# A block-diagonal 128x128 product done as four 64x64 products on the quarters of the array

## Chip, cores, metric

One core of a Trainium2 chip. The metric is device time in microseconds (us); each kernel ran several times and medians are given. The kernel before: 3359.38 us in the first three runs (3359.05 to 3360.88).

## The reference

```python
# x (8, 3008, 256); filt (1505, 256); w_in (256, 2048); w_out (2048, 256); all float32 in effect
X = np.fft.rfft(x, axis=1)
y = np.fft.irfft(X * (filt_r + 1j * filt_i)[None], n=3008, axis=1)
h = y.reshape(24064, 256) @ w_in
g = h * np.clip(h + 3, 0, 6) / 6
return g @ w_out
```

A Fourier transform along the tokens, a filter, the inverse transform, then an MLP.

## The kernel before

A transform of length 3008 = 47 x 64 goes in two stages. The first one, which the change touches, is a 64-point transform over n2 for each n1. The 48 (padded) values of n1 are n1 = 24 h + i with h = 0, 1. The two values of h lie on partitions 0 to 63 and 64 to 127, and the 24 values of i come in 6 chunks of 4. The weights `wa` are block-diagonal, the same 64x64 block twice, so half of the array multiplies by zero.

```python
wa[r, h * 64 + k2] = c                  # rows of h meet columns of h only; zero elsewhere
...
psF = pool("psF", 2, space=PSUM)        # two PSUM banks for all stages of the transform

def a_unit(b, i):                       # two values of i at a time
    c, r = divmod(i, XC // 2)
    ...
    ps = psF.tile([P, 2, D], FP32, name="psf", tag="f")
    nc.tensor.matmul(ps, wa, st["x", b, c][:, 2 * r:2 * r + 2, :], start=True, stop=True)
    nc.scalar.activation(out=st["t1", b, c][:, 2 * r:2 * r + 2, :], in_=ps, func=AXT.Copy)
    ...

def z_store(b, c):                      # to DRAM, where the next stage reads n1 along the partitions
    t = st.pop(("t1", b, c))
    for h in range(2):
        for ri in range(2):
            p0 = h * 64 + ri * 32
            r0 = ri * SL + h * H + c * XC
            nc.gpsimd.dma_start(z_d[b, :, r0:r0 + XC, :], t[p0:p0 + 32, :, :])

def down(b, m, jt):                     # second product of the MLP, four groups of tokens
    for q in ...:
        n = min(P, ntok(m) - q * P)     # 64 instead of 128 for q = 3 of the last block (448 tokens)
        nc.tensor.matmul(po[q // 2][0:n, q % 2, :], g[:, ds(q * P, n)], w_out[:, jt, :], ...)
```

The MLP of batch b runs in 96 slots: `up` (two matmuls of 512 columns), what the plan puts there of the transform of batch b + 1, `down` (four matmuls of 256). The first stage of batch b + 1 stands in every second slot from 0 to 22; the last stage of the inverse transform (`n_unit`) in slots 6, 8, 22, 24 and so on. Batch 0's transform runs ahead of the loop, beside the conversion of the weights. I call that stretch the start.

## Time and profile before

| | before |
|---|---|
| device time | 3359.38 us |
| profiled span | 3356.7 us |
| start, until the first MLP product | 237.07 us |
| one batch in the loop (batches 1 to 6 of the trace, first `up` to next first `up`) | 395.13 us |
| last batch, without a transform beside it | 345.57 us |
| tail, from the start of the last matmul to the end | 12.29 us |

The rows below the span are differences of start times read off the trace; together with the first batch (390.99) they fill the span. The batch is the row to read: inside it TensorE has no gap, so whatever lengthens or shortens TensorE's work changes it one to one. The prediction shows the lines.

Two words for what follows. A *record* is one matmul instruction in the trace; every f32 matmul of the code leaves two. A *visit* is a stretch in which TensorE works on less than the full 128x128 array, from the first such record to the next full-size one; what I call its price includes what the full-size records on both sides lose.

### The profile page before, as it was taken

To read this page: it belongs to the slowest core of one execution; us is meant where nothing else is said; L and a number is where in the kernel's file an instruction comes from. 1 tells how busy PE (TensorE), PEld (TensorE's weight loads), DVE (VectorE), ACT (ScalarE), POOL (GpSimd) and SP (SyncE) were. 2 spreads that over 40 slices of the span, in tenths; PEclk is the share of its full clock that TensorE was granted. 3 is DMA by queue.
4 is the path that set the end of the run, shared out by engine and by line. 5 is a ranking of instruction groups with operands and counts; after the bars stand their busy time and mean duration, and the time that the engine had idled before them with its cause. 6 is when DMAs were issued, how large, how long until landed. Compare 5 with 4: busy or idle time off the path is not lost.

```text
span 3356.7 us, 28371 instructions
## 1 busy us (share of the span) xinstructions
PE 3203.8 (95%) x11712; PEld 2117.0 (63%) x11712; DVE 919.8 (27%) x1413; ACT 740.8 (22%) x1137; POOL 218.2 (6%) x390
## 2 busy tenths in 40 slices
PE   1469999999999999999999999999999999999998
PEld 0246666666666676666675666666666666666665
DVE  2951232113321233112331133212332123311211
ACT  0012222222222222222222222222222222222221
POOL 2101000010001000010000100000000100000000
PEclk6579999999999999999999999999999999999999
DMA  8432121121212211021211212111111211010000
GB/s 149 140 100 77 32 60 39 37 58 47 55 29 62 52 45 44 24 74 47 65 28 44 62 37 63 32 55 46 52 44 29 74 43 43 24 36 19 19 7 12
DMA packets 76352, 168.20 MB, mean 50 GB/s; under 512 B 17410, under 2 KB 42244, under 8 KB 76032
## 3 DMA queue, kind: packets, MB, share of 16 engines
q0 software_dynamic: 32416, 86.55, 9.7%
q1 hardware_dynamic: 43808, 79.85, 9.2%
q8 instruction: 92, 1.51, 0.2%
q14 instruction: 36, 0.29, 0.0%
HBM read 91.29 MB, written 74.97 MB: 50 GB/s over the span
## 4 chain that ended last, share of the span: by engine, by line
PE 93%; DVE 3%; DMA 2%; issue 1%; POOL 0%; ACT 0%; SPq 0%; POOLq 0%; ACTq 0%
PE po L329 40%; PE psh L312 39%; PE psf L275 6%; PE psf L258 3%; PE psn L300 3%; PE psf L236 2%; DMA ft<-in_filt_i_dram 1%; DMA ft<-in_filt_r_dram 1%; DMA bits<-in_moe_w_in_dram 0%; DVE s L266 0%; DVE s L264 0%; DVE s L265 0%; DVE rest L213 0%; DVE rest L216 0%; DVE big L210 0%
## 5 line engine op out<-in xcount | busy, mean ns | idle before, releaser
L329 PE MATMUL po<-w_out,g 128*128 128x256 f32 (+1 forms) x6144 | 1471.9, 380 | 0.0
L312 PE MATMUL psh<-xn,w_in 128*128 128x512 f32 (+1 forms) x3072 | 1428.5, 587 | 0.0
L329 PEld LDWEIGHTS po<-w_out,g 128*128 128x128 f32 (+1 forms) x6144 | 1138.8, 188 | 398.9 <-issue 271.9
L317 DVE SCALAR_TENSOR_TENSOR g<-r,psh 128x512 f32<-128x512 f32 (+1 forms) x768 | 519.5, 676 | 2301.1 <-ACT r L316 2301.1
L316 ACT ACTIVATE r<-psh,half_c 128x512 f32<-128x512 f32 (+1 forms) x768 | 520.8, 678 | 2210.8 <-PE psh L312 2210.8
L312 PEld LDWEIGHTS psh<-xn,w_in 128*128 128x128 f32 x3072 | 573.8, 190 | 433.7 <-issue 399.2
L275 PE MATMUL psf<-s,wi 128*96 128x256 f32 x1024 | 261.6, 401 | 28.6 <-DVE s L266 28.1
L275 PEld LDWEIGHTS psf<-s,wi 128*96 128x96 f32 x1024 | 174.7, 173 | 131.9 <-issue 49.5
L236 PE MATMUL psf<-xc,wa 128*128 128x512 f32 x192 | 105.3, 639 | 76.2 <-ACT t L237 69.8
L258 PE MATMUL psf<-t,wb 96*128 96x256 f32 x512 | 139.3, 396 | 27.6 <-issue 19.0
L258 PEld LDWEIGHTS psf<-t,wb 96*128 96x128 f32 x512 | 98.5, 197 | 92.7 <-issue 67.5
L345 POOL DMA_DIRECT2D out_dram<-o x96 | 50.9, 535 | 1483.6 <-issue 1443.8
L300 PEld LDWEIGHTS psn<-wai,t 128*128 128x128 f32 x768 | 102.0, 194 | 52.6 <-issue 52.6
L280 ACT ACTIVATE t<-psf 96x512 f32<-96x512 f32 x128 | 75.9, 593 | 235.0 <-PE psf L275 235.0
L247 POOL DMA_DIRECT2D z_tmp<-t x192 | 93.4, 493 | 441.0 <-ACT t L237 414.9
L283 POOL DMA_DIRECT2D g_tmp<-t x64 | 44.6, 698 | 1069.6 <-ACT t L280 1068.6
L236 PEld LDWEIGHTS psf<-xc,wa 128*128 128x128 f32 x192 | 36.8, 203 | 117.8 <-ACT t L237 77.9
L300 PE MATMUL psn<-wai,t 128*128 128x128 f32 x768 | 102.6, 277 | 8.7 <-DMA t<-g_tmp 8.7
L264 DVE TENSOR_TENSOR s<-psf,ft 128x512 f32<-128x512 f32 x128 | 87.7, 685 | 15.2 <-PE psf L258 15.0
L266 DVE TENSOR_TENSOR s<-psf,ft 64x512 f32<-64x512 f32 x128 | 88.9, 695 | 1.8
L265 DVE TENSOR_TENSOR s<-psf,ft 64x512 f32<-64x512 f32 x128 | 87.4, 683 | 3.3
L237 ACT ACTIVATE t<-psf 128x512 f32<-128x512 f32 x96 | 56.9, 597 | 106.4 <-DMA z_tmp<-t 81.4
(34 smaller groups left out, 267.6 us busy)
## 6 DMA issues: line engine op xcount, KB each, us to landing
z_tmp<-t POOLq DMA_DIRECT2D x192, 128.0 KB, 3.6
t<-z_tmp SPq DMA_DIRECT2D x64, 384.0 KB, 3.9
g_tmp<-t POOLq DMA_DIRECT2D x64, 384.0 KB, 3.4
t<-g_tmp SPq DMA_DIRECT2D x192, 128.0 KB, 4.0
xc<-in_x_dram SPq DMA_DIRECT2D x88, 256.0 KB, 4.9
out_dram<-o POOLq DMA_DIRECT2D x88, 256.0 KB, 3.1
bits<-in_moe_w_in_dram POOLq DMA_DIRECT2D x8, 512.0 KB, 4.3
bits<-in_moe_w_out_dram POOLq DMA_DIRECT2D x8, 512.0 KB, 5.2
```

Of the source, the lines that this page charges most:

```text
L236: nc.tensor.matmul(ps, wa, st["x", b, c][:, 2 * r:2 * r + 2, :], start=True, stop=True)
L247: nc.gpsimd.dma_start(z_d[b, :, r0:r0 + XC, :], t[p0:p0 + 32, :, :])
L258: nc.tensor.matmul(ps[:, u, :], wb[k // KC][:, k % KC, :], st["t2", b, k // TC][:, k % TC, :], start=True, stop=True)
L264: nc.vector.tensor_tensor(out=s1, in0=ps, in1=f, op=ALU.mult)
L265: nc.vector.tensor_tensor(out=s2[0:HALF], in0=ps[0:HALF], in1=f[HALF:P], op=ALU.mult)
L266: nc.vector.tensor_tensor(out=s2[HALF:P], in0=ps[HALF:P], in1=f[0:HALF], op=ALU.mult)
L275: nc.tensor.matmul(ps[0:KR, u, :], wi[k // KC][:, k % KC, q, :], ss[q][:, u, :], start=(q == 0), stop=(q == 1))
L300: nc.tensor.matmul(ps[:, ts(q, P)], st["t4", b, m][:, q, ts(dh, P)], wai, start=True, stop=True)
L312: nc.tensor.matmul(ps[:, 0:w], w_in[:, dt, ts(jt, P)], xn[:, dt, 0:w], start=(dt == 0), stop=(dt == 1))
L316: nc.scalar.activation(out=r[:, 0:w], in_=ps[:, 0:w], func=AXT.Relu, bias=half_c, scale=1.0 / 6.0)
L317: nc.vector.scalar_tensor_tensor(out=g[:, 0:w], in0=r[:, 0:w], scalar=1.0, in1=ps[:, 0:w], op0=ALU.min, op1=ALU.mult)
L329: nc.tensor.matmul(po[q // 2][0:n, q % 2, :], g[:, ds(q * P, n)], w_out[:, jt, :], start=(jt == 0 and q % 2 == 0), stop=(jt == JT - 1 and ...
```

## The change

The intent is to use the idle half of the array. Each 64x64 block becomes a product on a quarter of its own: rows h, columns g, where g selects which two of the chunk's four values of i. All four can then work at once on different data. The PSUM tile is now one for each h, with g on the partitions, so the stores change too: eight of 64 KB in place of four of 128 KB. The chunk's products stand in one slot instead of two.

```diff
-            wa[r, h * 64 + k2] = c
+            wa[r, k2] = wa[r, 64 + k2] = c
 ...
-    def a_unit(b, i):
-        ...
-        ps = psF.tile([P, 2, D], FP32, name="psf", tag="f")
-        nc.tensor.matmul(ps, wa, st["x", b, c][:, 2 * r:2 * r + 2, :], start=True, stop=True)
-        nc.scalar.activation(out=st["t1", b, c][:, 2 * r:2 * r + 2, :], in_=ps, func=AXT.Copy)
+    def a_unit(b, c):
+        xc = st.pop(("x", b, c))
+        t = t1p.tile([P, 2, XC // 2, D], FP32, name="t1")
+        ps = [psF.tile([P, 2, D], FP32, name="psf", tag="f") for h in range(2)]
+        for g in range(2):
+            for h in range(2):
+                nc.tensor.matmul(ps[h][ts(g, 64)], wa[ts(h, 64), ts(g, 64)],
+                                 xc[ts(h, 64), 2 * g:2 * g + 2, :], start=True, stop=True)
+        for h in range(2):
+            nc.scalar.activation(out=t[:, h, :, :], in_=ps[h], func=AXT.Copy)
+        st["t1", b, c] = t

     def z_store(b, c):
-        for h in range(2):
+        for g in range(2):
             for ri in range(2):
-                p0 = h * 64 + ri * 32
-                r0 = ri * SL + h * H + c * XC
-                nc.gpsimd.dma_start(z_d[b, :, r0:r0 + XC, :], t[p0:p0 + 32, :, :])
+                p0 = g * 64 + ri * 32
+                r0 = ri * SL + c * XC + 2 * g
+                for h in range(2):
+                    nc.gpsimd.dma_start(z_d[b, :, r0 + h * H:r0 + h * H + 2, :], t[p0:p0 + 32, h, :, :])
 ...
-            for i in range(12):
-                at(t + 2 * i, a_unit, n, i)
-                if i % 2: ...                       # z_store, x_load at t + 2 * i + 1
+            for c in range(NB):
+                at(t + 4 * c, a_unit, n, c)
+                at(t + 4 * c + 2, z_store, n, c)    # and x_load
```

More of the change, by code (lines that the diff above doesn't have):

```diff
@@ L49, in _make_tables @@
             c, s = np.cos(th), np.sin(th)
-            wa[r, h * 64 + k2] = c
+            wa[r, k2] = wa[r, 64 + k2] = c
             wai[h * 64 + k2, r] = c * (2.0 if k2 else 1.0)
             if k2:
-                wa[r, h * 64 + 32 + k2] = -s
+                wa[r, 32 + k2] = wa[r, 96 + k2] = -s
                 wai[h * 64 + 32 + k2, r] = -2.0 * s
@@ L56, in _make_tables @@
                 alt = 1.0 - 2.0 * (n2 % 2)
-                wa[r, h * 64 + 32] = alt
+                wa[r, 32] = wa[r, 96] = alt
                 wai[h * 64 + 32, r] = alt
@@ L229, in x_load @@
         st["x", b, c] = t
-    def a_unit(b, i):
-        c, r = divmod(i, XC // 2)
-        if r == 0:
-            st["t1", b, c] = t1p.tile([P, XC, D], FP32, name="t1")
-        ps = psF.tile([P, 2, D], FP32, name="psf", tag="f")
-        nc.tensor.matmul(ps, wa, st["x", b, c][:, 2 * r:2 * r + 2, :], start=True, stop=True)
-        nc.scalar.activation(out=st["t1", b, c][:, 2 * r:2 * r + 2, :], in_=ps, func=AXT.Copy)
-        if r == XC // 2 - 1:
-            st.pop(("x", b, c))
+    def a_unit(b, c):
[9 more added lines that the diff above has]
+        st["t1", b, c] = t
     def z_store(b, c):
         t = st.pop(("t1", b, c))
-        for h in range(2):
+        for g in range(2):
             for ri in range(2):
-                p0 = h * 64 + ri * 32
-                r0 = ri * SL + h * H + c * XC
-                nc.gpsimd.dma_start(z_d[b, :, r0:r0 + XC, :], t[p0:p0 + 32, :, :])
+                p0 = g * 64 + ri * 32
+                r0 = ri * SL + c * XC + 2 * g
+                for h in range(2):
+                    nc.gpsimd.dma_start(z_d[b, :, r0 + h * H:r0 + h * H + 2, :], t[p0:p0 + 32, h, :, :])
     def t2_load(b, c):
@@ L362 @@
         for c in range(NB):
-            a_unit(0, 2 * c)
-            a_unit(0, 2 * c + 1)
+            a_unit(0, c)
             z_store(0, c)
@@ L403 @@
                 continue
-            for i in range(12):
-                at(t + 2 * i, a_unit, n, i)
-                if i % 2:
-                    c = i // 2
-                    at(t + 2 * i + 1, z_store, n, c)
-                    if c + 3 < NB:
-                        at(t + 2 * i + 1, x_load, n, c + 3)
+            for c in range(NB):
+                at(t + 4 * c, a_unit, n, c)
+                at(t + 4 * c + 2, z_store, n, c)
+                if c + 3 < NB:
+                    at(t + 4 * c + 2, x_load, n, c + 3)
             for c in range(3):
```

## The prediction

> **What bounds the kernel now.** I read the page first (busy shares, slices, chain, groups), then the timeline of PE in the loop, the groups with shapes kept apart, and the timelines of POOL and DVE in the start. From the page:
>
> ```profile
> PE 3203.8 (95%) x11712; PEld 2117.0 (63%) x11712; DVE 919.8 (27%) x1413; ACT 740.8 (22%) x1137; POOL 218.2 (6%) x390
> PE   1469999999999999999999999999999999999998
> ...
> PEclk6579999999999999999999999999999999999999
> ...
> PE 93%; DVE 3%; DMA 2%; issue 1%; POOL 0%; ACT 0%; SPq 0%; POOLq 0%; ACTq 0%
> ...
> L236 PE MATMUL psf<-xc,wa 128*128 128x512 f32 x192 | 105.3, 639 | 76.2 <-ACT t L237 69.8
> ```
>
> PE is full from the fourth slice on at full clock and is 93% of the chain. Up to about 240 us there is a start of another kind (transform of batch 0, conversion of weights). So in the loop each us of PE order is a us of the result; in the start it is not. The stage that changes (L236) is 105 us of busy PE: 96 matmuls in the code (8 batches x 12), 192 records, so an f32 matmul is two pairs of weight load and matmul. Its 70 us of waiting for ACT lie in the start (13 waits in all, the longest 62 us). Only batches 1 to 7 pay in the loop: 7 x 6 = 42 chunks of two matmuls. The timeline of PE in the loop:
>
> ```profile
> 243.18 1.02 PE L236 MATMUL psf<-xc,wa 128*128 128x512 f32 x2
> 244.04 1.89 PE L329 MATMUL po<-w_out,g 128*128 128x256 f32 x8
> 245.76 1.88 PE L312 MATMUL psh<-xn,w_in 128*128 128x512 f32 x4
> 247.48 1.89 PE L329 MATMUL po<-w_out,g 128*128 128x256 f32 x8
> ```
>
> Starts count, not durations (they overlap). L236 takes 244.04 - 243.18 = 0.86 us for two records, 0.43 each; L312 takes 1.72 for four, again 0.43; L329 1.72 for eight of half width. No gap anywhere. A chunk costs 4 x 0.43 = 1.72 us, and 42 chunks 72 us: even removing the stage would gain 2.15%, and halving it 36 us, 1.1%.
>
> **What the skill says.** First, the Trainium skill, "TensorE: Matmul & The Clock Gate", Back-to-back issue gap, gives N / 2.4 + 2.5 ns, 216 ns for 512 columns; the trace has 430 for f32, so each of the two records streams its columns twice. The time follows the columns streamed, not rows or outputs used: a 64x64 product alone is no cheaper than a 128x128 one. Second, "TensorEngine Tiling (Array Packing)", Key Properties: tiles work in parallel, but changing the tiling mode drains the engine. Third, the first page, The mechanism (packing small matmuls): matmuls start and end strictly in program order, and a weight load runs beside matmuls in flight only where the row group differs. Of running side by side this trace shows nothing. Of changing mode it does, because the last token block has a product with 64 columns of weights:
>
> ```profile
> 597.71 1.77 PE L312 MATMUL psh<-xn,w_in 128*128 128x448 f32 x4
> 599.31 2.03 PE L329 MATMUL po<-w_out,g 128*128 128x256 f32 x8
> 601.28 1.77 PE L312 MATMUL psh<-xn,w_in 128*128 128x448 f32 x4
> ...
> L329 PEld LDWEIGHTS po<-w_out,g 128*64 128x64 f32 x256 | 24.4, 134 | 42.5 <-issue 42.5
> ```
>
> The first three are the timeline in the block of 448 tokens, the last the group of 64-column loads. Without a change of mode L312 would take 1.72 x 448/512 = 1.505 us and L329 1.72, together 3.23. From 597.71 to 601.28 it is 3.57: **0.34 us for one visit** to the 64-column mode, with two records in it. The two narrow records start 0.27 us apart (600.70 and 600.97 in a narrower window) where wide ones of 256 columns start 0.215 apart, so about 0.05 us is a second load that is not hidden in this mode. A visit is thus about 0.29 us, plus 0.05 for each further load into a tile just in use. This agrees with the second page in that leaving and re-entering the full mode costs something.
>
> **The change, part by part.**
> 1. PE, per chunk. Removed: two matmuls, 4 records, 1.72 us. Added: four matmuls, 8 records of the same 512 columns, 0.43 each, in the order (rows 0, columns 0), (rows 1, columns 0), (0,1), (1,1). The built program has 5952 matmuls against 5856, and 2 records each. All four quarters at once would be 2 x 0.43. But each product is a pair of records on one quarter, next to each other in the queue, and the second must wait for the first; as order is strict, nothing passes it. So: first of A; second of A beside first of B; second of B beside first of C; second of C beside first of D; second of D. That is **5 steps of 0.43 = 2.15 us**, not 2. Add 4 unhidden second loads, 4 x 0.05 = 0.2, and a visit, 0.29: 2.65 us. Against 1.72: +0.93 us a chunk, x 42 = **+39 us**.
> 2. Both PSUM buffers of the tag are taken in one slot instead of one in every second slot. In slot 8 of each batch the last-stage product (L300) stands in front and holds one of them: its eviction takes 0.6 us plus some 0.2 to start, while the second quarter product would want the buffer after 0.6. About 0.3 us, x 7 = +2 us. ACT has the same two evictions of 0.60 a chunk; it is 22% busy, so nothing.
> 3. Stores. Eight per chunk of 64 KB in place of four of 128 KB, 192 more POOL issues of 0.49 us = 94 us of POOL, which has 6% busy; in the loop the reader of this data comes four slots (over 14 us) after the last store is given, against 3.6 us to land. Nothing there. In the start the last chunk's stores are on the path:
>
> ```profile
> 105.14 0.56 POOL L188 DMA_DIRECT2D bits<-in_moe_w_in_dram x1 [3.86 <-DVE rest L213]
> 105.70 2.09 POOL L247 DMA_DIRECT2D z_tmp<-t x4
> ...
> 116.78 0.69 DVE L264 TENSOR_TENSOR s<-psf,ft 128x512 f32<-128x512 f32 x1 [3.96 <-PE psf L258]
> ```
>
> Timelines of POOL and DVE: four stores end at 107.8, the read starts at 110.7, and DVE, which then sets the pace until 206 us, has waited 3.96 us for it. Eight stores end 2 us later: **+2 us**. The chunks before are paced by DVE (6.5 us each, against 8 x 0.5 + 0.6 of POOL), so nothing more. The PE work of batch 0 hides beside DVE.
>
> Sum: 39 + 2 + 2 = +43 us, 3402. Loads of the next quarter might not be pulled ahead in full, which makes each of three steps up to 0.1 us longer (up to 12 us); I add 3 for that: **3405 us**, +1.4%.
>
> **The rivals.**
> - *No overlap at all*: f32 with its double passes, or this mode, lets only one quarter run. Then 8 x 0.43 + 7 x 0.05 + 0.29 = 4.10 us a chunk, +2.38, x 42 = +100, with the 4 us above 3463 us, +3.1%. For it: no record of the kernel before shows two matmuls together. Against: the skill measured such overlap, if not in f32. 23%.
> - *Full overlap*: all first records together, then all second ones: 2 x 0.43 + 0.05 + 0.29 = 1.20 us, -0.52, x 42 = -22, plus 4: 3341 us, -0.5%. It is what the change intends. Against: the pairs stand one after another and order is strict. 7%.
> - *A heavier visit*: changing rows and columns might drain longer than changing columns alone. Each 0.1 us more is 4 us; 0.6 us more would be needed to reach +2%. 5%.
> - *The start or DMA moves the result*: more and smaller packets where DMA is busiest (share 8 of 10 in the first slice). The stores of the first chunk stand behind filter and weight loads and may be some us later, but DVE's conversions do not wait for them. A few us at most.
>
> **Range and chances.** Main case 3402 to 3420, 65%; serial about 3463, 23%; full overlap about 3341, 7%; the rest between. Range 3378 to 3468. The line for +2% is 3426.6, for -2% 3292. Slower by over 2%: 23% plus a heavy visit, 0.28. Faster by over 2% would take more than the whole loop share of the stage: 0.01. Within 2%: 0.71.
>
> **What would show it.** In the changed kernel's PE timeline inside the loop: from the first record of the quarter products to the next L329 or L312-type product 2.65 us (main), 4.1 (serial) or 1.2 (full); second records of one quarter start within some 10 ns of first records of the next (main), all starts 0.43 or more apart (serial), four starts together (full). 384 records in the group. POOL at about 600 instructions, with 8 stores a chunk; first DVE product in the start at about 118.8 instead of 116.78; DMA and ACT still far from full. The prediction is wrong if PE idles in the loop on ACT or DMA by more than some us, if the visit costs much over 0.3 us, or if the start moves by more than about 5 us.

## The result

The changed kernel takes **3335.95 us** (3335.33 to 3336.33, 4 runs) against 3359.22 us (3357.64 to 3360.88, 4 runs): ratio 0.993, 95% interval 0.9916 to 0.9944. A ratio is the mean of one kernel's fast runs over the mean of the other's of the same rounds, so not quite the ratio of the medians. Results are correct. The prediction said 3405 and a range from 3378 to 3468: the sign was wrong. The mean granted clock is 0.973 before and 0.987 after, but only the start differs: from the first MLP product on it is 1.00 in both, and the last batch takes 345.57 us in both.

From the page of the changed kernel, busy time by engine and the group of the quarter products (its line is now L239):

```profile
PE 3185.7 (96%) x11904; PEld 2090.9 (63%) x11904; DVE 920.4 (28%) x1413; ACT 737.3 (22%) x1137; POOL 315.3 (9%) x582
...
L239 PE MATMUL psf<-xc,wa 64*64 64x512 f32 x384 | 67.0, 673 | 75.6 <-ACT t L242 70.6
```

Twice the records (384 against 192) in 67.0 us of busy time instead of 105.3. Records that run together count once in busy time. The waiting for ACT before it, 70.6 against 69.8 us, is the same: it lies in the start. The timeline of TensorE in the loop shows one visit (start and length in us, then the group; L317 is `up`, L334 `down`):

```profile
246.88 1.88 PE L317 MATMUL psh<-xn,w_in 128*128 128x512 f32 x4
248.69 1.09 PE L239 MATMUL psf<-xc,wa 64*64 64x512 f32 x8
249.71 1.99 PE L334 MATMUL po<-w_out,g 128*128 128x256 f32 x8
251.54 1.88 PE L317 MATMUL psh<-xn,w_in 128*128 128x512 f32 x4
```

Eight records of 512 columns from 248.69 to 249.71, **1.02 us**; at 0.43 us each, one after another, they would take 3.44. The neighbours pay for the change of mode: L317 takes 1.81 instead of 1.72 up to the visit, and L334 1.83 instead of 1.72 after it. In all, 246.88 to 251.54 is 4.66 us, less 3.44 for the neighbours: a chunk costs 1.22 us instead of 1.72. The starts of the records of another such visit, read off the trace (ns from the first; A to D are the quarters in the order of the code, "load" is the weight load of a record):

```
load A1 -2  load B1 5   load C1 12  load D1 18      first records of A, B, C, D start at 0, 7, 13, 20
load 2nd records   53  60  67  73                   second records            start at 480, 487, 493, 500
next product (full array) starts at 1019
```

All four first records run together, then all four second ones. That is the rival that the prediction called full overlap and gave 7%. Where the time went, from the same starts as in the table above:

| us | before | after | difference |
|---|---|---|---|
| start | 237.07 | 235.15 | -1.92 |
| seven batches with a transform beside them | 390.99 + 6 x 395.13 | 388.85 + 6 x 392.88 | -15.6 |
| last batch | 345.57 | 345.57 | 0 |
| tail | 12.29 | 7.53 | -4.8 |
| span | 3356.7 | 3334.4 | -22.3 |

Two things are left to explain. The loop gave back 15.6 us, not 42 x 0.50 = 21; and 4.8 us came from a tail that the change seems not to touch.

For the first: in slot 8 the visit follows a product of the last stage (L305). The timelines of TensorE and of its weight loads there:

```profile
264.48 1.05 PE L305 MATMUL psn<-wai,t 128*128 128x128 f32 x8
265.47 1.84 PE L239 MATMUL psf<-xc,wa 64*64 64x512 f32 x8
267.24 1.13 PE L334 MATMUL po<-w_out,g 128*128 128x256 f32 x4
```

```profile
265.47 0.19 PEld L239 LDWEIGHTS psf<-xc,wa 64*64 64x64 f32 x2
266.22 0.20 PEld L239 LDWEIGHTS psf<-xc,wa 64*64 64x64 f32 x6 [0.57 <-ACT xn L306]
```

This visit takes 1.77 us. Two loads are issued at once and six 0.75 us later, after ACT has emptied the bank that L305 used. The same lines answer a second question, namely what the queue looks like. The two early loads are both of quarter A (its first and its second record), so in the queue the two records of a product stand together, ahead of the wait that belongs to B. (A build of the kernel has them so: A1 A2 B1 B2 C1 C2 D1 D2.) Yet in an undisturbed visit B1, C1 and D1 start 7 to 20 ns after A1, and A2 only at 480 ns. **They pass A2.**

### The profile page after: what moved, and what is told of

It is laid out like the page before. It is cut to its first block, busy times and chain, and to the rows that moved or that the text cites. A ratio compares the mean times of both kernels' runs of the same rounds, so it can differ in the third digit from the quotient of the medians.

```text
span 3334.4 us, 29079 instructions
## 1 busy us (share of the span) xinstructions
PE 3185.7 (96%) x11904; PEld 2090.9 (63%) x11904; DVE 920.4 (28%) x1413; ACT 737.3 (22%) x1137; POOL 315.3 (9%) x582
## 4 chain that ended last, share of the span: by engine, by line
PE 93%; DVE 3%; DMA 2%; issue 1%; POOL 1%; ACT 0%; SPq 0%; POOLq 0%; ACTq 0%
PE po L334 41%; PE psh L317 39%; PE psf L280 6%; PE psf L263 3%; PE psn L305 3%; DMA ft<-in_filt_i_dram 2%; PE psf L239 1%; DMA z_tmp<-t 0%; POOL z_tmp L252 0%; DVE s L271 0%; DVE s L269 0%; DVE s L270 0%; DVE rest L216 0%; DVE rest L213 0%; DVE big L210 0%
## 5 line engine op out<-in xcount | busy, mean ns | idle before, releaser
L334 PE MATMUL po<-w_out,g 128*128 128x256 f32 (+1 forms) x6144 | 1476.2, 381 | 0.0
L317 PE MATMUL psh<-xn,w_in 128*128 128x512 f32 (+1 forms) x3072 | 1428.6, 587 | 0.0
L334 PEld LDWEIGHTS po<-w_out,g 128*128 128x128 f32 (+1 forms) x6144 | 1134.4, 188 | 405.8 <-issue 278.8
L317 PEld LDWEIGHTS psh<-xn,w_in 128*128 128x128 f32 x3072 | 574.0, 190 | 433.9 <-issue 399.6
L252 POOL DMA_DIRECT2D z_tmp<-t x384 | 190.4, 503 | 260.9 <-ACT t L242 235.2
L239 PE MATMUL psf<-xc,wa 64*64 64x512 f32 x384 | 67.0, 673 | 75.6 <-ACT t L242 70.6
L305 PEld LDWEIGHTS psn<-wai,t 128*128 128x128 f32 x768 | 102.2, 194 | 52.5 <-issue 52.5
L305 PE MATMUL psn<-wai,t 128*128 128x128 f32 x768 | 102.8, 278 | 8.7 <-DMA t<-g_tmp 8.7
L239 PEld LDWEIGHTS psf<-xc,wa 64*64 64x64 f32 x384 | 13.8, 140 | 117.4 <-ACT t L242 80.3
```

The lines of the kernel that those rows point to most:

```text
L239: nc.tensor.matmul(ps[h][ts(g, 64)], wa[ts(h, 64), ts(g, 64)], xc[ts(h, 64), 2 * g:2 * g + 2, :], start=True, stop=True)
L252: nc.gpsimd.dma_start(z_d[b, :, r0 + h * H:r0 + h * H + 2, :], t[p0:p0 + 32, h, :, :])
L305: nc.tensor.matmul(ps[:, ts(q, P)], st["t4", b, m][:, q, ts(dh, P)], wai, start=True, stop=True)
L317: nc.tensor.matmul(ps[:, 0:w], w_in[:, dt, ts(jt, P)], xn[:, dt, 0:w], start=(dt == 0), stop=(dt == 1))
```

## The experiments

The theory after the result: (1) each quarter works off its own line of records, so the time of a visit is the number of records on the busiest quarter x 0.43 us, plus about 0.34 us for changing the mode there and back; (2) slot 8 loses 0.75 us to the PSUM bank; (3) tail and start have to do with the stores. The rivals stand in the expectations.

### Quarter products one slot later

```diff
-                at(t + 4 * c, a_unit, n, c)
-                at(t + 4 * c + 2, z_store, n, c)        # and x_load
+                at(t + 4 * c + 1, a_unit, n, c)
+                at(t + 4 * c + 3, z_store, n, c)        # and x_load
```

> The changed kernel with the quarter products one slot later (slots 4c+1 instead of 4c), so that none stands right behind a last-stage product. Theory (a chunk's visit costs 1.02 us from first to next start, and the seven chunks of slot 8 cost 1.77 because the second quarter waits 0.75 us for the PSUM buffer of the product in front): every visit 1.02, seven of them 0.75 us shorter, 3335.9 - 5.3 = 3330.7 us. Rival (the 1.77 come from changing the mode right behind the short 128-column products, whatever the buffers): the visits near last-stage products stay long, or the time moves into ACT, and the time stays within 1.5 us of 3335.9.

Measured: 3330.35 us (3328.54 to 3331.29), ratio to before 0.9912 (0.9898 to 0.9927). A batch takes 392.13 instead of 392.88 us, that is 0.75 less, and all 42 visits last 1.02 us. The slot of L305 is now followed by an undisturbed visit one slot later:

```profile
262.12 1.05 PE L305 MATMUL psn<-wai,t 128*128 128x128 f32 x8
...
266.55 1.09 PE L239 MATMUL psf<-xc,wa 64*64 64x512 f32 x8
267.57 1.78 PE L334 MATMUL po<-w_out,g 128*128 128x256 f32 x7
```

Point (2) holds: the change's own placement cost 7 x 0.75 = 5 us.

### How far the queue reaches: half-products of one quarter next to each other, or far apart

```diff
             for h in range(2):
-                nc.tensor.matmul(ps[h][ts(g, 64)], wa[ts(h, 64), ts(g, 64)],
-                                 xc[ts(h, 64), 2 * g:2 * g + 2, :], start=True, stop=True)
+                for u in range(2):              # in the second kernel this loop is outermost
+                    nc.tensor.matmul(ps[h][ts(g, 64), u, :], wa[ts(h, 64), ts(g, 64)],
+                                     xc[ts(h, 64), 2 * g + u, :], start=True, stop=True)
```

> The changed kernel with each quarter product cut into two of 256 columns, the two of a quarter next to each other in the queue: four records of one quarter (0.215 us each) stand ahead of the first record of the next quarter. Theory A (each quarter works off its own line, and what stands behind other records of another quarter is reached at once): the four quarters still start within some 30 ns of each other and a visit stays near 1.05 us, time 3336 to 3338. Theory B (only one record may be pending on a quarter, a further one stops the queue): the first record of the next quarter starts about 0.48 us after that of the one before, a visit takes about 2.5 us, 42 x 1.4 = +60, time near 3395. Rival (the strict order of my prediction): 13 steps of 0.215, a visit of 3.0 us, time near 3420.

> The same 16 records of 256 columns as in the run before, but in the order: first halves on all four quarters, then second halves. Theories A and B: a visit near 1.05 us, time 3336 to 3338, so the difference to the run before is the price of the order in the queue alone. Strict order: first halves 5 steps, second halves 4 more, 9 x 0.215 + 0.3, a visit of 2.2 us, time near 3388.

Measured: 3336.08 us (3334.83 to 3339.38) with the halves next to each other and 3335.65 (3333.89 to 3339.04) with them apart; ratios 0.9932 and 0.993. One visit of the first of the two kernels, and the starts of its 16 records:

```profile
247.96 1.11 PE L240 MATMUL psf<-xc,wa 64*64 64x256 f32 x16
249.01 1.99 PE L335 MATMUL po<-w_out,g 128*128 128x256 f32 x8
```

```
first records of A, B, C, D    0   13   26   40
second records               266  280  293  306
third                        482  495  509  522
fourth                       698  711  725  738     next product 1044
```

Three waiting records of A stand ahead of B's first one in the queue, and B starts 13 ns after A. That all four records of A do stand ahead of B shows in a slot 8 of this kernel: there A's start at 0, 266, 482 and 698 ns, and B's first one, after its wait for the bank, at 756. With the other order the step is 7 ns and the visit 1.02 us: the order in the queue costs 0.02 us. So theory A holds as far as three waiting records; neither a strict order (3.0 us) nor one waiting record per quarter (2.5 us) is left.

### Only the two quarters of the diagonal

The kernel before, with its layout and its stores, but each product split into the two blocks of its diagonal, and a chunk's four in one visit.

```diff
+        for r in range(2):
+            for h in range(2):
+                nc.tensor.matmul(ps[r][ts(h, 64)], wa[ts(h, 64), ts(h, 64)],
+                                 xc[ts(h, 64), 2 * r:2 * r + 2, :], start=True, stop=True)
```

> The kernel before (its layout, its four stores of 128 KB), with the chunk as four 64x64 products in one visit, but only on the two quarters of the diagonal (rows and columns 0 to 63, rows and columns 64 to 127). Theory (the time is the number of records on the busiest quarter x 0.43 plus 0.34 for a visit): 4 x 0.43 + 0.34 = 2.06 us a chunk against 1.72 before, 42 x 0.34 = +14, time about 3373 (slot 8 adds nothing, since the wait is hidden behind the first pair). Rival (64x64 products are cheap in themselves, whatever their number at once): 3336 to 3345. Strict order: 1 + ... 7 steps of 0.43 at most, 3.3 us, time near 3425.

Measured: 3372.42 us (3370.51 to 3373.62), ratio 1.0036 (1.002 to 1.0053). A batch takes 397.20 us, 2.07 more than before, or 0.345 for each of its six chunks; 0.34 was expected. A visit on TensorE's timeline:

```profile
251.95 1.93 PE L237 MATMUL psf<-xc,wa 64*64 64x512 f32 x8
253.82 1.99 PE L331 MATMUL po<-w_out,g 128*128 128x256 f32 x8
```

The same eight records take 1.87 us on two quarters and 1.02 on four. The products are not cheap in themselves; what pays is that four run at once. With two at once the four steps take as long as before, and the visit comes on top. Point (1) holds.

### The stores, both ways

Four stores a chunk in the changed kernel (each still in pieces of 2 KB), and eight in the kernel before:

```diff
-                for h in range(2):
-                    nc.gpsimd.dma_start(z_d[b, :, r0 + h * H:r0 + h * H + 2, :], t[p0:p0 + 32, h, :, :])
+                rows = z_d[b, :, ri * SL:(ri + 1) * SL, :].rearrange("k (h r) d -> k h (r d)", h=2)
+                lo = (c * XC + 2 * g) * D
+                nc.gpsimd.dma_start(rows[:, :, lo:lo + 2 * D],
+                                    t[p0:p0 + 32, :, :, :].rearrange("p h a d -> p h (a d)"))
```

> The changed kernel with its eight stores of 64 KB a chunk merged into four of 128 KB (each still in pieces of 2 KB). So far the profiles with 192 such stores end with 12.29 us after the start of the last matmul and begin the loop at 236 to 237 us; those with 384 stores end with 7.5 us and begin it at 232.7 to 235.2. Theory (some 7 us of the gain are not from the quarters but from the number of stores, in the tail after the last matmul, and in the start): tail back to 12.3, loop start about 236.5, batches unchanged at 392.9, time about 3342. Rival (the tail goes with the instructions of TensorE or with the size of the pieces): tail 7.5, time 3336.

```diff
-                nc.gpsimd.dma_start(z_d[b, :, r0:r0 + XC, :], t[p0:p0 + 32, :, :])
+                for r in range(0, XC, 2):
+                    nc.gpsimd.dma_start(z_d[b, :, r0 + r:r0 + r + 2, :], t[p0:p0 + 32, r:r + 2, :])
```

> The kernel before with each of its four stores a chunk split into two of 64 KB, the rest untouched: the store part of the change alone. Theory: tail 7.5 instead of 12.3, loop start 2 to 4 us earlier, batches unchanged at 395.13, time 3360 - 4.8 - 3 = about 3352. My prediction's step 3 had +2 us for this part (3362). Rival (tail goes with TensorE): 3360.

Measured: 3335.57 us (3335.08 to 3336.48) and 3354.04 us (3352.54 to 3355.89) against 3359.63 for before in the same rounds; ratios 0.9932 and 0.9988 (0.9975 to 1.0). In both, batches are unchanged and the tail is 7.52 us. So the first expectation failed: with four stores again the tail stays short. Not the number of stores but how they are cut goes with it: 2 KB pieces in both, 4 KB in before (by the element size in the store instructions; the DMA queue's packets do not show the cut: its 20324 packets of 4 KB are the same number in before, in the changed kernel and in these two). The second came out near its 3352, and it shows that the tail has nothing to do with TensorE: the store part of the change alone makes 5.6 us between the medians, 4.8 of them in the tail. Its interval touches 1.0, so the time alone hardly settles it; the traces do, with tails of 7.51 to 7.53 us in all seven kernels with 2 KB pieces throughout and 12.29 in all three with 4 KB. Where the 4.8 us lie is seen in the instructions at the program's end, here POOL's drains of before, changed kernel, and before with eight stores (min/median/max, ns):

```profile
L462 POOLq DRAIN  x3: 46/108/9362, 3346.6 to 3356.5; - x3
```

```profile
L464 POOLq DRAIN  x3: 46/108/4601, 3329.0 to 3334.1; - x3
```

```profile
L463 POOLq DRAIN  x3: 46/108/4595, 3346.9 to 3352.0; - x3
```

The longest of the three, the first behind POOL's last store, takes 9.36 us or 4.60 us, and the kernel ends 0.8 us after it. It is not the last transfer that is waited for: the last packet ends 5.25 us after the start of the last matmul in before and 5.27 in the changed kernel. As for the start, it was 235.54 us here with four stores and 237.03 with eight, the other way round than expected, and among all kernels with eight stores in every batch it lies between 232.70 and 237.10. So the stores don't explain it, and the theory's point (3) about the start fell; whether the 1.9 us of the changed kernel are more than scatter stays open. Sorted by the products instead, the six kernels with all four quarters have 232.70 to 237.10 us and the other six 236.32 to 238.46, with one profile each: a leaning, and no run shows a cause.

### Are small pieces good as such?

The kernel before, with pieces of 2 KB only from some batch on:

```diff
+                w = 2 if b >= 7 else XC            # the other kernel: b >= 4
-                nc.gpsimd.dma_start(z_d[b, :, r0:r0 + XC, :], t[p0:p0 + 32, :, :])
+                for r in range(0, XC, w):
+                    nc.gpsimd.dma_start(z_d[b, :, r0 + r:r0 + r + w, :], t[p0:p0 + 32, r:r + w, :])
```

> The kernel before with the stores split into pieces of 2 KB in the last batch only (768 more pieces than its 6144, where the split of all batches has 6144 more). It asks whether the shorter tail after the last matmul (7.52 us where all stores are in 2 KB pieces, 12.29 where they are in 4 KB pieces, whatever the matmuls and whatever the number of store instructions) comes from small pieces as such. Theory (small pieces as such, near the end): 7.5 us. Rival (it is a matter of the count of pieces, as of a position in a ring): anything, not in proportion; most likely 12.3 again or another value.

> The same with the stores split in the last four batches (3072 more pieces). Theory (small pieces as such): 7.5 us as in the other run. Proportion to the count: about 10 us here and 11.7 in the other. Rival (position): the two runs differ without order.

Measured (one look each): tails of 9.75 and 10.25 us. In the first, POOL issues the last store 4.6 us after the start of the last matmul (1.7 in before) and then drains in 3.88 us; in the second 1.7 and 7.33 us. So small pieces as such are not the reason, nor a proportion to their count (11.7 and 10 were expected for it). The tail moves irregularly with the count of pieces, and in one case POOL's delay lies ahead of the store instead of behind it, with no instruction in the profile. Some work of POOL's that falls due now and then would fit, but this is a guess: no run shows such work. The cause stays open.

### The price of a visit by itself

Before has 128 visits of its own: the product with 64 columns of weights in each of the 16 slots of the last block of tokens, 8 batches. Here that product takes 128 columns, the last 64 zeroed, so it stays in the full mode. The second kernel has it on top of the later slots.

```diff
+        if w < 512:
+            nc.vector.memset(g[:, w:512], 0.0)
 ...
-            n = min(P, ntok(m) - q * P)
-            nc.tensor.matmul(po[q // 2][0:n, q % 2, :], g[:, ds(q * P, n)], w_out[:, jt, :],
+            nc.tensor.matmul(po[q // 2][:, q % 2, :], g[:, ds(q * P, P)], w_out[:, jt, :],
```

> The kernel before without its 128 visits to the 64-column mode: in the last token block the fourth product takes all 128 columns, of which the last 64 are zeroed by a small memset on VectorE; the forward stage is untouched. Theory (a visit costs 0.34 us on the path, whatever the work in it): 128 x 0.34 = 44 us less, time about 3316; a batch 389.7 instead of 395.13 us. Rival (the 0.34 us are the slowness of the narrow product itself or of the shorter matmuls beside it, or the memset delays the product by a wait): above 3340.

> The quarter products one slot later (as in the run of that change alone, 3330.4) and no visit to the 64-column mode in the last token block. Theory: the two gains add, 3330.4 - 44 = 3286 us; a batch 392.13 - 5.47 = 386.7 us. Rival (they overlap, as visits of one mode pay for those of the other): nearer to 3310.

Measured: 3315.82 us (3313.86 to 3316.57), ratio 0.9872, and **3287.40 us** (3286.69 to 3289.01), ratio 0.9789 (0.9776 to 0.9802). Batches take 389.67 and 386.67 us. TensorE in the last block of the first of the two:

```profile
593.08 1.67 PE L312 MATMUL psh<-xn,w_in 128*128 128x448 f32 x4
594.58 1.89 PE L330 MATMUL po<-w_out,g 128*128 128x256 f32 x8
596.31 1.67 PE L312 MATMUL psh<-xn,w_in 128*128 128x448 f32 x4
```

A slot is 596.31 - 593.08 = 3.23 us, where it was 3.57: 0.34 less, though the product is twice as wide. A batch is 5.46 us shorter, 16 x 0.34. A visit costs about as much in all three kinds measured here: 0.34 us with the narrow product, 0.345 on the diagonal, 1.22 - 2 x 0.43 = 0.36 on four quarters. The two gains add up. The kernel with both is the fastest found, and of its gain of 72 us the visits avoided have 44, the quarters 21 (7 x 3.0 us between 395.13 and 392.13) and the tail 4.8.

## Why the prediction was wrong

- **What bounds the kernel, and the ceiling: right.** TensorE's order set the loop, a chunk was worth 1.72 us, and nothing of the stage could give more than 72 us. ACT and DMA stayed out of the way, as step 2's last sentence and step 3 had it for the loop.
- **The failed step is in part 1**: "the second must wait for the first; as order is strict, nothing passes it", hence "5 steps". The first half is right, within a quarter. The second half is not: the next quarter's records do pass it, at once, and past three waiting records just as well. In its place the visit takes two steps, 1.02 us. A chunk is 1.72 - 1.22 = 0.50 us cheaper instead of 0.93 dearer. The step rested on one sentence of the Trainium skill, "TensorE: Matmul & The Clock Gate", The mechanism: "MATMULs are pc-monotone in start AND end". The trace of before could not confirm it, and I said so, but gave the opposite case 7% all the same. The page does not say on which mix of records it was measured; one record on each tile would look the same with either rule. (Nor does it name the data type of the packed products that it measured.)
- **Loads: wrong in a small term.** "4 unhidden second loads" are not there. The second loads start at 53 to 73 ns, under the first records. Unhidden is only the first load of the visit: second records start at 480 = 53 + 427. The 0.05 us that I read off two narrow records in before was that first load; a visit has it once, and part 1 counted it four times.
- **The visit: right.** 0.34 us was read from before's timeline, and the run without those visits returned 43.8 us between the medians, against 128 x 0.34 = 43.5. With it and the right number of steps the rival "full overlap" had 1.20 us a chunk; 1.22 was measured. That its total of 3341 us lies so near to 3336 is partly luck: it had a gain of 20 us in the loop, where 15.6 came, and a loss of 2 in the start, where start and tail together gained 6.7.
- **Step 2: the right place, the wrong size.** 0.3 us was predicted for slot 8, 0.75 is what the later slots took away. The size came from the failed step: in the five-step picture B wants its bank 0.6 us after A, in truth 7 ns after.
- **Step 3: wrong by its size in the start, and blind at the end.** With eight stores in place of four the wait of VectorE for the last of them grew by 0.6 to 0.8 us (changed kernel 3.77 to 4.39, before 3.96 to 4.76), not by 2. And the product behind it came at 113.79 us, not at about 118.8: the conversions ahead of it had ended 3.4 us earlier than in before, which no run explains. The tail of POOL's drain gave 4.8 us, a fifth of the gain, and nothing in the prediction looked at the end of the program.

The sum, on the profiled spans: predicted +39, +2, +2. Measured: 35 undisturbed chunks x -0.50 = -17.5, 7 chunks of slot 8 at 0.093 + 1.77 + 0.103 = 1.97 us (lead-in, visit, first load behind it) x +0.25 = +1.7, together -15.8 against -15.6 measured by batches; start -1.9, tail -4.8.

## What to carry to other kernels

Products that fit a quarter of the array paid here with four quarters at work in one visit and lost with two: count records on the busiest quarter, and add the visit's 0.34 us. Look for changes of mode that nobody meant, such as one narrow product at a ragged end: padding it to full width was worth more here (44 us) than the packing (23). And when a prediction rests on an ordering rule that no view of the case at hand shows, give the opposite rule a real share of the chances.

## What the Trainium skill lacked or had wrong

- "TensorE: Matmul & The Clock Gate", The mechanism: matmuls start in program order. Across quarters they do not: B's first record starts 7 ns after A's first, and A's second, which stands ahead of it in the queue, at 480 ns. With three waiting records of A ahead, B starts 13 ns after A. (The page's step of some 4 ns between tiles was 7 ns here.)
- "TensorEngine Tiling (Array Packing)", Key Properties: changing the mode drains the engine, without a figure. Here a visit costs 0.34 us: about 93 ns before it, 53 for the first load of 64 columns, 92 behind the last record, 103 for the first load of 128 columns after it. (The starts: 523 ns from the last full-size record to the visit's first, of which that record has 430; second record at 480 and not 427; next product at 1019, where the last record, from 500, has 427; then 320 to the record after it, which is else 216 away.)
- "TensorE: Matmul & The Clock Gate", Back-to-back issue gap, does not tell f32 apart; an f32 matmul of 512 columns takes 2 x 0.43 us, four times the page's 216 ns. "FP8 and Floating Point Precision", TensorE Precision Notes, has the reason, four passes for true FP32, and agrees.
- No page says that POOL's drain at the end of a program with DMAs issued from POOL can take microseconds: 9.36 us in before, 4.60 with its stores cut in pieces of 2 KB, 3.88 and 7.33 with only some cut.
